# Float32 attention times values for two batches, with row sums from columns of ones, and weight conversion in 512-column pieces

## The chip, the cores and the metric

The kernel runs on one core of one Trainium2 chip. Five engines run their own instruction streams side by side: TensorE (PE in the profile, its weight loads PEld), VectorE (DVE), ScalarE (ACT), GpSimd (POOL) and SyncE (SP), which here issues the DMAs. They wait for each other through semaphores. The metric is the device time of one execution in microseconds (us); the median of several executions counts.

## The reference

Block-causal attention over 8 batches, 8 heads, 576 positions and 64 dimensions, followed by a two-layer feed-forward over all 4608 tokens, everything in float32:

```python
scores = scale * np.matmul(q, k.transpose(0, 1, 3, 2))
scores = np.where(block_i >= block_j, scores, -1000000000.0)      # blocks of 64
scores = scores - np.max(scores, axis=-1, keepdims=True)
attn = np.exp(scores)
attn = attn / (np.sum(attn, axis=-1, keepdims=True) + 1e-09)
x = np.matmul(attn, v)                     # to (4608, 512), heads side by side
h = x @ w_in                               # w_in 512 x 2048
g = np.where(h >= 1, h, np.where(h <= -1, 0.0, (h + 1) ** 2 / 4))
out = g @ w_out                            # w_out 2048 x 512
```

## The kernel before

**Precision.** TensorE multiplies float32 in several passes and a reduced type, float32r, in one. To keep the accuracy, an operand a is split into a high half (a rounded to float32r) and a low half (a minus the high half, again float32r), and a product is the sum of two or three float32r products. So nearly every tile exists twice: `xh` and `xl` for the attention output x, `wih` and `wil` for `w_in`, `gh` and `gl` for the activations g. `w_out` is split once, written to DRAM (`wo_split`) and read back for each use.

**Attention.** The unit is a pair: two heads of one batch, 32 pairs in all, four to a batch. `Pair` holds its methods and `attention_steps` runs each pair in eight steps. Queries are split by `split_q` (its last instruction is on line 292) in the fourth step of the pair before. A head has the score groups (0, 0), (0, 1), (0, 2) for key and query tiles of 128, and both heads share one group for the last 64 positions. For each group `scores` (or `scores_last`) multiplies (lines 371 and 374), takes row maxima (394, DVE), exponentials with their row sums (398, ACT), adds 1e-9 and inverts the sums (`inverse`, 380 and 381), and multiplies the rows of P by them (404, or 430 for the last). `turn` transposes P through PSUM (`transposed`, 441 or 443) and `split` copies it to SBUF: the high half by ACT (434), the low half by DVE (436). `weighted` multiplies it by the values (480).

**Three kinds of batches.** Batch 0 is `plain`: P stays float32, has no low half, and is multiplied by float32 values. The tile `vs` has the values of one head in one half of its columns and zeros in the other, so both heads add up in one PSUM bank (`both`), from which ACT takes `xh` (515) and DVE `xl` (516). All later batches split P in two halves and multiply by `vsr`, which has the high half of the values on one side and their low half on the other; `add_halves` (502 on ACT, 503 on DVE) adds the two sides into `x32`, and `store_x` (545, 546) splits that into `xh` and `xl`. From batch 3 on (`HOP = 3`), P makes a hop through DMA into a float32r tile (`as_float32r`, tile `prr`) before it is transposed, so that the transposes run in float32r. The tiles of a hop come from the pools `conv` and `conv2`, which also serve the weight conversion and the output tiles `ob`.

**Weight conversion.** `convert` splits a piece of 128 rows by `CW = 256` columns in three stages, one for each later step: a load (`bits`), two ACT operations (164, 165) and three DVE operations (166, 169, 172); then an addition on POOL (178) and a copy on ACT (180); then a subtraction on POOL (182). There are 64 pieces. Odd ones among the first 32 borrow tiles from the feed-forward's pool.

**Feed-forward.** Nine chunks of 512 tokens by 16 blocks of 128 hidden columns. A block is `ffn_in`, twelve 512-column matmuls into `ph` (626) and then ACT (635), DVE (636, 639), ACT (640) and POOL (641), and `ffn_out`, twelve more into four banks `po` (650, 655). From step `START = 36`, the middle of batch 1's first pair, one of these half blocks is issued with each attention step, and what is left after the last pair runs alone.

**What sets the order.** The code is written step by step, and a scheduler of the tile framework places the instructions on the engines' queues, by the buffers and operands that each needs. Engines run their queues in order. PSUM has eight banks: three work banks (`ps_w`), one for `ph`, four for `po`. Before `START` the work takes turns over the `po` banks too (`work_bank`), afterwards it has the three alone.

## Time and profile before

| | |
|---|---|
| runs | 1288.21, 1285.29, 1286.38 us; median 1286.38 |
| profiled execution | 1285.23 us, its span 1283.5 us |
| mean granted TensorE clock | 0.983 |
| PE busy | 1207.2 us, 94% of the span |
| PEld busy | 1018.7 us, 79% |
| DVE busy | 888.4 us, 69% |
| ACT busy | 766.3 us, 60% |
| POOL busy | 472.2 us, 37% |
| DMA | 188.44 MB, mean 147 GB/s |

The page divides the span into 40 slices and gives the busy share of each engine in tenths. A row of the grouped views reads: line, engine, operation, output tile <- input tiles, shapes, count | busy us, mean ns of one | idle time of the engine just before, and what ended it. The windows view gives the busy time of every engine between two moments. A row of waits names who waited for whom, the total in us, how often, and the longest.

### The profile page before, as it was taken

What the parts mean: (1) busy time and instruction counts of PE and PEld (TensorE: products, weight loads), DVE (VectorE), ACT (ScalarE), POOL (GpSimd) and SP (SyncE); (2) the same over time, 40 slices, a digit from 0 to 9 for tenths busy, and PEclk for the clock granted to TensorE, in tenths of its full rate; (3) what the DMA queues carried; (4) which work ended last, traced back from release to release, by engine and by line L of the source; (5) the groups of instructions that cost most, each with busy time, mean ns of one, the idle gap of its engine ahead of it and who ended that gap; (6) DMA issues with size and microseconds to landing.
All of it is one profiled execution on the core that took longest, in us unless ns stands there. A gap on an engine that the chain in (4) does not pass through costs nothing.

```text
span 1283.5 us, 20410 instructions
## 1 busy us (share of the span) xinstructions
PE 1207.2 (94%) x6496; PEld 1018.7 (79%) x6496; DVE 888.4 (69%) x2204; ACT 766.3 (60%) x1855; POOL 472.2 (37%) x466
## 2 busy tenths in 40 slices
PE   5877787899999999999999999999999999999998
PEld 4666665688888888888888888888888888888886
DVE  8998999877677777677777777777777767322222
ACT  6878676666666666666666666666666655322222
POOL 3545766633333333333333333333333332222222
PEclk9889999999999999999999999999999999999999
DMA  5656555434333545555444644464545443333432
GB/s 152 175 151 180 170 186 177 145 125 140 97 106 111 189 143 153 160 159 178 147 155 154 187 137 152 153 189 148 159 146 186 156 142 120 115 99 99 132 99 99
DMA packets 136812, 188.44 MB, mean 147 GB/s; under 512 B 61040, under 2 KB 87664, under 8 KB 136704
## 3 DMA queue, kind: packets, MB, share of 16 engines
q1 hardware_dynamic: 136704, 187.13, 47.2%
q8 instruction: 52, 0.85, 0.3%
q14 instruction: 56, 0.46, 0.1%
HBM read 120.59 MB, written 17.83 MB: 108 GB/s over the span
## 4 chain that ended last, share of the span: by engine, by line
PE 70%; DVE 13%; ACT 8%; issue 4%; DMA 2%; POOL 1%; SPq 1%; ACTq 0%; POOLq 0%; DVEq 0%
PE ph L626 26%; PE po L650 16%; PE po L655 8%; PE ps_av L480 7%; PE ps_s L371 3%; PE ps_s L374 3%; ACT pr L398 3%; PE ps_t L441 3%; PE ps_qk L327 2%; DVE pr L404 2%; ACT qb L331 2%; DVE nm L394 2%; DVE work L169 1%; PE ps_t L443 1%; DVE work L172 1%
## 5 line engine op out<-in xcount | busy, mean ns | idle before, releaser
L641 POOL TENSOR_TENSOR gl<-t,gh 128x512 fp32r<-128x512 f32 x144 | 187.2, 1300 | 577.5 <-ACT gh L640 310.8
L650 PE MATMUL po<-wo,gh 128*128 128x512 f32 x1152 | 299.7, 403 | 0.1
L650 PEld LDWEIGHTS po<-wo,gh 128*128 128x128 f32 x1152 | 210.6, 190 | 40.3 <-ACT gh L640 0.6
L626 PE MATMUL ph<-xh,wih 128*128 128x512 f32 x576 | 238.2, 414 | 1.7 <-DVE t L639 1.7
L636 DVE SCALAR_TENSOR_TENSOR t<-t 128x512 f32<-128x512 f32 x144 | 112.9, 784 | 183.1 <-ACT t L635 181.0
L626 PE MATMUL ph<-xl,wih 128*128 128x512 f32 x576 | 227.4, 395 | 1.1 <-DVE xl L516 1.1
L626 PE MATMUL ph<-xh,wil 128*128 128x512 f32 x576 | 227.9, 396 | 0.0
L635 ACT ACTIVATE t<-ph 128x512 f32<-128x512 f32 x144 | 86.0, 597 | 155.2 <-PE ph L626 155.2
L398 ACT ACTIVATE pr<-ps_s,nm 128x128 f32<-128x128 f32 (+3 forms) x256 | 134.2, 529 | 63.1 <-DVE nm L394 62.8
L655 PE MATMUL po<-wo,gl 128*128 128x512 f32 x576 | 155.4, 391 | 0.0
L394 DVE TENSOR_REDUCE nm<-ps_s 128x1 f32<-128x128 f32 (+3 forms) x256 | 123.6, 485 | 45.2 <-PE ps_s L374 43.6
L371 PE MATMUL ps_s<-ka,qa 68*128 68x288 f32 (+4 forms) x384 | 123.6, 336 | 20.5 <-ACT pr L398 12.8
L640 ACT CAST gh<-t 128x512 fp32r<-128x512 f32 x144 | 90.0, 625 | 84.6 <-DVE t L639 83.0
L626 PEld LDWEIGHTS ph<-xh,wil 128*128 128x128 f32 x576 | 109.4, 190 | 24.5
L434 ACT CAST pb<-ps_t 128x512 fp32r<-128x512 f32 (+1 forms) x140 | 77.5, 553 | 84.8 <-PE ps_t L441 65.5
L317 POOL TENSOR_TENSOR vsr<-vn,vsr 128x256 fp32r<-128x256 f32 (+1 forms) x112 | 82.9, 750 | 119.9 <-ACT vsr L316 119.9
L655 PEld LDWEIGHTS po<-wo,gl 128*128 128x128 f32 x576 | 108.4, 188 | 23.4
L626 PEld LDWEIGHTS ph<-xl,wih 128*128 128x128 f32 x576 | 109.9, 191 | 20.4 <-DVE xl L516 1.4
L626 PEld LDWEIGHTS ph<-xh,wih 128*128 128x128 f32 x576 | 109.4, 190 | 20.3 <-DVE t L639 2.0
L374 PE MATMUL ps_s<-kb,qb 128*128 128x288 f32 (+4 forms) x384 | 121.8, 323 | 0.0
L436 DVE TENSOR_TENSOR pb<-ps_t,pb 128x512 fp32r<-128x512 f32 (+1 forms) x140 | 88.1, 629 | 40.5 <-ACT pb L434 40.5
L404 DVE TENSOR_SCALAR pr<-pr,sm 128x128 f32<-128x128 f32 (+3 forms) x256 | 110.3, 451 | 3.6
(95 smaller groups left out, 2039.1 us busy)
## 6 DMA issues: line engine op xcount, KB each, us to landing
wo<-wo_split SPq DMA_DIRECT2D x144, 512.0 KB, 3.4
prr<-pr SPq DMA_DIRECT2D x80, 192.0 KB, 2.6
prr<-pr SPq DMA_DIRECT2D x60, 256.0 KB, 2.4
out_dram<-ob SPq DMA_DIRECT2D x36, 256.0 KB, 4.0
qn<-in_q_dram SPq DMA_DIRECT2D x32, 256.0 KB, 2.9
kn<-in_k_dram SPq DMA_DIRECT2D x32, 256.0 KB, 3.0
bits<-in_moe_w_in_dram SPq DMA_DIRECT2D x32, 256.0 KB, 3.1
bits<-in_moe_w_out_dram SPq DMA_DIRECT2D x32, 256.0 KB, 3.1
```

Source lines behind the costliest of these rows:

```text
L371: nc.tensor.matmul(ps, qa[:KA, j, c0 : c0 + P], ka[:KA, j, k0 : k0 + n], start=first, stop=False)
L374: nc.tensor.matmul(ps, qb[:, j, c0 : c0 + P], kb[:, j, k0 : k0 + n], start=False, stop=last)
L394: nc.vector.tensor_reduce(out=nm[:, i : i + 1], in_=ps[:, cs], axis=AX.X, op=ALU.max, negate=True)
L398: nc.scalar.activation(pr[:, cs], ps[:, cs], AF.Exp, bias=nm[:, i : i + 1], scale=1.0, accum_out=sm[:, i : i + 1],)
L404: nc.vector.tensor_scalar_mul(pr[:, cs], pr[:, cs], sm[:, i : i + 1])
L480: nc.tensor.matmul(ps[:, lo_col:], vt, x, start=first and i == 0 and m == 0, stop=last and i == len(parts) - 1 and m == len(mov) - 1,)
L626: nc.tensor.matmul(ph, w[:, cc, fs], x[:, cc, xs], start=(cc == 0 and i == 0), stop=(cc == NCC - 1 and i == 2),)
L636: nc.vector.scalar_tensor_tensor(out=t_, in0=t_, scalar=1.0, in1=t_, op0=ALU.min, op1=ALU.mult)
L640: nc.scalar.copy(gh, t_)
L641: nc.gpsimd.tensor_tensor(out=gl, in0=t_, in1=gh.bitcast(F32), op=ALU.subtract)
L650: nc.tensor.matmul(po[tt], gh[:, ts_], wo[:, w, :], start=(fc == 0 and w == 0), stop=False)
L655: nc.tensor.matmul(po[tt], gl[:, ts_], wo[:, 0, :], start=False, stop=fc == NFC - 1)
```

## The change

- **Two plain batches.** `PLAIN = 2`: batches 0 and 1 keep P in float32. Batches 2 to 7 hop (`self.hop = not self.plain`), so batch 2 hops too.
- **P unnormalised in plain batches.** The exponentials are neither summed nor divided. The half of `vs` beside a head's values holds ones, so the matmul of P and `vs` gives the weighted sum in one half of the partitions and the row sum in the other. The tiles `vs` and `pc` are made once; their unused rows are zero. The two heads no longer share a PSUM accumulation. The new `divided` copies the sums plus 1e-9 to the other half of the partitions (ACT), inverts them (DVE, 256 or 320 columns) and multiplies (DVE) into `x32`. `store_x` then serves all batches.
- **Evictions.** A P without a low half, in groups 1, 2 and the last, is copied out of PSUM by DVE and no longer by ACT; group 0 stays on ACT.
- **Conversion** in pieces of 512 columns, 32 in all, with the first operations in place. `w_in` lies in four groups of 512 columns, whose last one takes the place of the pool `early` when that closes. Twelve pieces (24 half as large before) are spread over the first 36 steps, then one is issued in each step, two ahead in both cases.
- **Hops** are one DMA each, also for the 576 columns of the last group, into tiles of the one pool `conv` (two tags of two buffers); `ob` takes its tiles from there too.

```diff
-    BORROW = 32
-    CW = 256
+    CW = 512
+    NG = DF // CW
-    HOP = 3
+    PLAIN = 2
...
-    conv = ctx.enter_context(tc.tile_pool(name="conv", bufs=3))
-    conv2 = ctx.enter_context(tc.tile_pool(name="conv2", bufs=3))
+    conv = ctx.enter_context(tc.tile_pool(name="conv", bufs=2))
...
+    late["early"] = late["pool"].enter_context(tc.tile_pool(name="early", bufs=2))
...
+        pool = late["early"] if n % 2 and late["early"] else conv
+        bits = pool.tile([P, CW, 2], I32, tag="bits", name="bits")
+        mag = pool.tile([P, CW], U32, tag="mag", name="mag")
...
-        nc.scalar.mul(top, bits[:, :, 1].bitcast(F32), 2.0**-112)
+        nc.scalar.mul(top, top, 2.0**-112)
...
     def as_float32r(src):
-        for c0 in range(0, src.shape[1], TCH):
...
+        n = src.shape[1]
+        hops["n"] += 1
+        if n > TCH or hops["n"] % 2:
+            dst = conv.tile([P, 2 * TCH], F32R, tag="bits", name="prr")
+        else:
+            dst = conv.tile([P, TCH], F32R, tag="mag", name="prr")
+        nc.sync.dma_start(dst[:, :n].bitcast(F32), src)
...
-            self.plain = b == 0
+            self.plain = b < PLAIN
-            self.hop = b >= HOP
+            self.hop = not self.plain
...
+                    nc.gpsimd.memset(both[:, 0, :, 1, :], 1.0)
+                    nc.gpsimd.memset(both[:, 1, :, 0, :], 1.0)
...
-                    accum_out=sm[:, i : i + 1],
-                )
-            self.inverse(sm[:, :m])
-            for i, cs in enumerate(cols):
-                nc.vector.tensor_scalar_mul(pr[:, cs], pr[:, cs], sm[:, i : i + 1])
+                    accum_out=None if self.plain else sm[:, i : i + 1],
+                )
+            if not self.plain:
+                self.inverse(sm[:, :m])
+                for i, cs in enumerate(cols):
+                    nc.vector.tensor_scalar_mul(pr[:, cs], pr[:, cs], sm[:, i : i + 1])
...
         def split(self, ps, hi, lo=None):
+            if lo is None and ps.shape[1:] == hi.shape[1:] and len(ps.shape) > 2:
+                nc.vector.tensor_copy(hi, ps)
+                return
...
-        def both(self, c0, parts):
...
+        def divided(self, ps, heads, c0):
+
+            n = ps.shape[1] // len(heads)
+            total = att1.tile([P, G1], F32, tag="xtmp", name="xtmp")
+            halves = [slice(j * D, (j + 1) * D) for j in range(2)]
+            for i, j in enumerate(heads):
+
+                nc.scalar.activation(
+                    total[halves[j], :n], ps[halves[1 - j], i * n : (i + 1) * n], AF.Identity,
+                    bias=EPS, scale=1.0,
+                )
+            rows_ = slice(heads[0] * D, (heads[-1] + 1) * D)
+            nc.vector.reciprocal(total[rows_, :n], total[rows_, :n])
+            for i, j in enumerate(heads):
+                nc.vector.tensor_tensor(
+                    out=self.x32[halves[j], c0 : c0 + n], in0=ps[halves[j], i * n : (i + 1) * n],
+                    in1=total[halves[j], :n], op=ALU.mult,
+                )
...
         def attn_v(self, j):
-            if self.plain:
-                return self.both(G0, self.parts) if j else None
             ps = work_bank("ps_av")[:, :G1]
             self.weighted(ps, j, self.parts(j))
-            self.add_halves(ps, j, G0)
+            self.divided(ps, (j,), G0) if self.plain else self.add_halves(ps, j, G0)
...
-        if i < START:
-            want = (i + 1) * EARLY // START
-        else:
-            want = max(
-                EARLY + (i - START + 1) * (NFC // GROUP * PART - EARLY) // (2 * NFC - 4 * GROUP),
-                ((i - START) // (2 * GROUP) + 1) * PART,
-            )
+        want = (i + 1) * EARLY // START if i < START else EARLY + i - START + 1
```

How the queues change, at two places. On DVE in batch 0, where the second head's first groups of a pair are handled, there stood before (`work` is a conversion's tile, `sm` the row sums, `pr` the rows of P):

```order
L380 TENSOR_SCALAR sm<-sm 128x2
L169 TENSOR_SCALAR work<-work 128x256
L381 RECIPROCAL sm<-sm 128x2
L169 TENSOR_SCALAR work<-work 128x256
L404 TENSOR_SCALAR pr<-pr,sm 128x128
L404 TENSOR_SCALAR pr<-pr,sm 128x256
L380 TENSOR_SCALAR sm<-sm 128x1
L172 SCALAR_TENSOR_TENSOR work<-work 128x256
L381 RECIPROCAL sm<-sm 128x1
L172 SCALAR_TENSOR_TENSOR work<-work 128x256
L404 TENSOR_SCALAR pr<-pr,sm 128x384
L394 TENSOR_REDUCE nm<-ps_s 128x1
```

The small sums, their reciprocals and the multiplies of P stand among the conversion. At the same place of the third pair there stands now (`pb` is the transposed P, `ps_t` its PSUM bank, `ps_av` the bank of P times values, `xtmp` the sums, `x` the tile x32, `mag` and `bits` a conversion's tiles):

```order
L540 RECIPROCAL xtmp<-xtmp 64x320
L454 COPY pb_724<-ps_t 128x3x128
L542 TENSOR_TENSOR x_725<-ps_av,xtmp 64x320
L180 SCALAR_TENSOR_TENSOR mag<-bits,mag 128x512
L410 TENSOR_REDUCE nm<-ps_s 128x1 x2
L540 RECIPROCAL xtmp<-xtmp 128x256
L454 COPY pb_724<-ps_t 128x4x128
L542 TENSOR_TENSOR x_725<-ps_av,xtmp 64x256 x2
L410 TENSOR_REDUCE nm<-ps_s 128x1
```

What normalised P before the transposes now divides after the product, in fewer and wider instructions, and the copies of P stand beside them.

On PE in batch 1, the second head's product of P and the values in the pair's last columns was, before:

```order
L480 MATMUL ps_av<-pb_1375,vsr_110 128x320
L480 MATMUL ps_av<-pb_1376,vsr_110 128x320
L480 MATMUL ps_av<-pb_1375,vsr_110 128x320
L480 MATMUL ps_av<-pb_1376,vsr_110 128x320
L480 MATMUL ps_av<-pb_1375,vsr_110 128x320
L480 MATMUL ps_av<-pb_1376,vsr_110 128x320
L480 MATMUL ps_av<-pb_1375,vsr_110 128x192
L480 MATMUL ps_av<-pb_1376,vsr_110 128x192
L480 MATMUL ps_av<-pcs_107,vsr_110 128x64
L480 MATMUL ps_av<-pcs_108,vsr_110 128x64
L626 MATMUL ph<-xh,wih 128x512
```

and is now, with the first feed-forward matmuls behind it in both:

```order
L501 MATMUL ps_av<-pb_1196,vs 128x320 x3
L501 MATMUL ps_av<-pb_1196,vs 128x192
L501 MATMUL ps_av<-pc,vs 128x64
L654 MATMUL ph<-xh,wih_96 128x512
L654 MATMUL ph<-xl,wih_96 128x512
```

Ten float32r matmuls of a high and a low half have become five float32 matmuls. From the fourth batch on the rows of PE, DVE and POOL are the same ones in the same order in both kernels; on ACT a few copies of output tiles stand one or two places later, and on SP the hop of a last group is one DMA where there were two.

More of the change, by code (lines that the diff above doesn't have):

```diff
@@ L505, in add_halves @@
             )
-        def both(self, c0, parts):
-            n = (G0, G1)[c0 > 0]
-            ps = work_bank("ps_av")[:, :n]
-            for j in range(2):
-                self.weighted(ps, j, parts(j), j == 0, j == 1)
-            at = self.b * S + c0
-            hi = xh[:, self.hp, at : at + n]
-            nc.scalar.copy(hi, ps)
-            nc.vector.tensor_tensor(
-                out=xl[:, self.hp, at : at + n], in0=ps, in1=hi.bitcast(F32), op=ALU.subtract
-            )
+        def divided(self, ps, heads, c0):
[13 more added lines that the diff above has]
+                    in1=total[halves[j], :n], op=ALU.mult,
+                )
         def attn_v_first(self):
-            if self.plain:
-                return self.both(0, self.parts_first)
             ps = work_bank("ps_av")
@@ L568, in attention_steps @@
                 cur.turned(False, 1)
-                cur.load("v")
+                if not cur.plain:
+                    cur.load("v")
             if old:
@@ L578, in attention_steps @@
                 old.store_x()
+            if cur and cur.plain:
+                cur.load("v")
             if not cur:
```

124 lines of the change are left out of this document (60 added, 64 removed).

## The prediction

> **What bounds the kernel now.** I read the page's slices first, then cut the span at one recurring instruction and asked for the busy time of each stage.
>
> ```profile
> PE   5877787899999999999999999999999999999998
> PEld 4666665688888888888888888888888888888886
> DVE  8998999877677777677777777777777767322222
> ```
>
> Up to the eighth slice, about 257 us, DVE is the full engine and PE is not; afterwards PE is full. The cut is the query split, one for each pair of heads, issued in the fourth step of the pair before. The second, sixth and ninth stand at 23.6, 109.3 and 253.9 us, the thirteenth at 390:
>
> ```profile
> 109.29 0.73 DVE L292 SCALAR_TENSOR_TENSOR qs<-qn,qs 128x576 fp32r<-128x576 f32 x1
> 253.87 0.75 DVE L292 SCALAR_TENSOR_TENSOR qs<-qn,qs 128x576 fp32r<-128x576 f32 x1
> ```
> ```profile
> 23.60:109.30 85.70, 67.64 (x361) 53.46 (x361) 76.77 (x231) 72.83 (x208) 44.70 (x58) 0.90 0.58 167
> 109.30:253.90 144.60, 113.89 (x566) 91.56 (x564) 132.72 (x306) 100.35 (x269) 92.82 (x105) 0.93 0.55 172
> 253.90:390.00 136.10, 131.69 (x739) 113.58 (x740) 98.39 (x250) 85.34 (x206) 45.66 (x43) 0.99 0.39 117
> 390.00:1031.00 641.00, 636.37 (x3630) 545.83 (x3629) 467.97 (x1190) 415.04 (x986) 219.35 (x197) 1.00 0.51 159
> ```
>
> Columns: length, then busy time (with count) of PE, PEld, DVE, ACT and POOL, then the granted TensorE clock. Stage A, 85.7 us, is four pairs of the first batch without the feed-forward: DVE 76.77 (90%), PE 67.64 (79%). Stage B, 144.6 us, is three pairs with the feed-forward and most of the weight conversion: DVE 132.72 (92%), PE 113.89 (79%) at a clock of 0.93. From 253.9 us a pair costs 136.1/4 = 34.0 us, from 390 us 641/19 = 33.7, with PE busy 97 to 99%. So the sum is made on DVE in A and B, with PE as the floor. What DVE does there, A first, then B:
>
> ```profile
> L404 DVE TENSOR_SCALAR pr<-pr,sm 128x128 f32<-128x128 f32 (+3 forms) x30 | 18.8, 648 | 0.2
> ...
> L166 DVE TENSOR_SCALAR work<-work 128x256 f32<-128x256 f32 x22 | 11.2, 515 | 4.4 <-ACT work L164 4.4
> L172 DVE SCALAR_TENSOR_TENSOR work<-work 128x256 uint32<-128x256 uint32 x21 | 10.5, 501 | 0.1
> L169 DVE TENSOR_SCALAR work<-work 128x256 uint32<-128x256 uint32 x21 | 8.5, 411 | 0.1
> ...
> L381 DVE RECIPROCAL sm<-sm 128x1 f32<-128x1 f32 (+1 forms) x27 | 4.2, 154 | 0.2
> L380 DVE TENSOR_SCALAR sm<-sm 128x1 f32<-128x1 f32 (+1 forms) x27 | 4.0, 147 | 0.7 <-ACT pr L398 0.6
> L516 DVE TENSOR_TENSOR xl<-ps_av,xh 128x256 fp32r<-128x256 f32 (+1 forms) x7 | 3.1, 446 | 1.0 <-ACT xh L515 1.0
> ```
> ```profile
> L172 DVE SCALAR_TENSOR_TENSOR work<-work 128x256 uint32<-128x256 uint32 x39 | 24.4, 629 | 0.5
> L169 DVE TENSOR_SCALAR work<-work 128x256 uint32<-128x256 uint32 x39 | 22.5, 585 | 0.4
> L404 DVE TENSOR_SCALAR pr<-pr,sm 128x384 f32<-128x384 f32 (+3 forms) x25 | 16.7, 688 | 0.1
> L166 DVE TENSOR_SCALAR work<-work 128x256 f32<-128x256 f32 x38 | 14.9, 394 | 2.4 <-ACT work L164 2.3
> ...
> L436 DVE TENSOR_TENSOR pb<-ps_t,pb 128x512 fp32r<-128x512 f32 (+1 forms) x15 | 9.4, 628 | 1.6 <-ACT pb L434 1.6
> ...
> L503 DVE TENSOR_TENSOR x<-ps_av,xtmp 64x320 f32<-64x320 f32 (+1 forms) x12 | 5.4, 452 | 3.3 <-ACT xtmp L502 3.1
> ...
> L381 DVE RECIPROCAL sm<-sm 128x1 f32<-128x1 f32 (+1 forms) x22 | 3.4, 155 | 0.2
> ...
> L436 DVE TENSOR_TENSOR pa<-ps_t,pa 128x384 fp32r<-128x384 f32 x6 | 3.3, 548 | 0.7 <-ACT pa L434 0.7
> L380 DVE TENSOR_SCALAR sm<-sm 128x1 f32<-128x1 f32 (+1 forms) x21 | 3.1, 147 | 0.7 <-ACT pr L398 0.6
> ```
>
> **What goes from DVE.** In both batches the normalising of P and its small reciprocals go: 18.8 + 4.2 + 4.0 in A, 16.7 + 3.4 + 3.1 in B. In A the low half taken straight from PSUM (3.1) moves to POOL, which is half idle there (44.7 of 85.7). In B the low halves of P (9.4 + 3.3) and the adding of halves (5.4) go. Together 30.1 in A and 41.3 in B.
>
> **Conversion.** The nearest rows for 512 columns are these, and they also price what is added:
>
> ```profile
> L636 DVE SCALAR_TENSOR_TENSOR t<-t 128x512 f32<-128x512 f32 x144 | 112.9, 784 | 183.1 <-ACT t L635 181.0
> ...
> L404 DVE TENSOR_SCALAR pr<-pr,sm 128x512 f32<-128x512 f32 x64 | 36.4, 569 | 1.0
> ...
> L381 DVE RECIPROCAL sm<-sm 128x1 f32<-128x1 f32 x160 | 25.0, 156 | 2.8
> ...
> L665 DVE COPY ob<-po 128x512 f32<-128x512 f32 x18 | 12.1, 685 | 4.1 <-PE po L655 3.7
> L381 DVE RECIPROCAL sm<-sm 128x2 f32<-128x2 f32 x64 | 10.4, 163 | 1.7
> ```
>
> A piece is two TENSOR_SCALARs and one two-source operation: 2 x 569 + 784 = 1.92 us at 512 columns. At 256 it costs 1.43 in A (515 + 501 + 411) and 1.61 in B, because DVE meets more company there; I scale the large one by 1.61/1.43 in B, 2.2 us. By the new table 11 pieces fall in A and 18 in B. So 30.2 becomes 21.1 (A) and 61.8 becomes 39.6 (B): 9.1 and 22.2 us off. If the source with a step of two costs DVE its better rate, the two TENSOR_SCALARs go at the 685 of the PSUM copy: 0.23 us a piece, 2.5 and 4 us back.
>
> **What comes to DVE.** Per pair: three PSUM copies of 512 columns (685), two of 384 (548, the same width out of PSUM), a small one of some 0.3: 3.5 us; four multiplies at 452 ns: 1.8 us. In A (four pairs) 14.0 + 7.2, in B (three) 10.5 + 5.4. Then the term I know least: a reciprocal over 256 columns and two over 320 for each pair, where the kernel before has only one and two columns. The two rows differ by 7 ns for one more column. That is the high end: 163 + 254 x 7 = 1.94 us and 2.39 us, 6.7 us a pair. The low end is one column at a time as a PSUM copy goes, (685 - 548)/128 = 1.07 ns: 0.43 and 0.50, 1.4 us a pair. I take the high end, since it is the only row of the operation itself.
>
> The Trainium skill (VectorE: DVE Perf Modes, First, the fixed hardware budget) says that the reciprocal runs through an iterative divide with a repeat count of 8. Read as eight cycles of its 0.96 GHz a column, an estimate from that page, it is 7.9 us a pair and the result would be some 8 us later than my sum; the 2-column row, 7 ns dearer and not 8.3, leaves it open, and both lie in the forecast's own range.
>
> **Stage A.** 76.8 - 30.1 - 9.1 + 14.0 + 7.2 + 26.9 = 85.7 us of DVE; at the 92% that DVE reached in B this takes 93.3, **+7.6**. ACT does not take over: it hands the P copies to DVE and stops reading accumulators, against four short copies a pair.
>
> **Stage B.** 132.7 - 41.3 - 22.2 + 10.5 + 5.4 + 20.2 = 105.3 us of DVE, 115 at 92%. PE is now as near. Its own change:
>
> ```profile
> L480 PE MATMUL ps_av<-pb,vsr 128*128 128x320 f32 x448 | 71.5, 302 | 1.2 <-ACT pr L398 1.2
> L480 PE MATMUL ps_av<-pa,vsr 128*128 128x256 f32 x224 | 31.4, 282 | 0.5 <-DVE pa L436 0.3 <-ACT pr L398 0.2
> ...
> L480 PE MATMUL ps_av<-pb,vs 128*128 128x320 f32 (+1 forms) x64 | 17.5, 417 | 0.6 <-ACT pb L434 0.6
> L480 PE MATMUL ps_av<-pa,vs 128*128 128x256 f32 (+1 forms) x32 | 9.0, 408 | 0.0
> ```
>
> Seven batches of two float32r halves take 102.9 us, 14.7 each; one batch in float32 takes 26.5. So the second batch pays 11.8 us more on PE, 3.0 a pair: 34.0 + 3.0 = 37.0, and 111 us for three pairs is the floor. With two engines at 111 and 105 neither runs free; I take 120 us, PE at 92%: **-24.6**.
>
> **The rest.** The third batch now goes through DRAM to float32r like the later ones: 33.7 instead of 34.0 a pair, **-1.2**. Before A, three pieces stand for four and the first pair loses its normalising: 0 within 2 us. From the fourth batch on PE, DVE and POOL have the same rows in the same order, so nothing is added. Sum: +7.6 - 24.6 - 1.2 = -18.2 on the profiled execution of 1285.2 us, which lies 1.2 under the median 1286.4. **Forecast 1267 us.**
>
> **Rival 1: the wide reciprocal streams.** At 1.4 us a pair DVE has 64.4 us in A and 89.4 in B, and PE is the bound in both: A 67.64/0.95 = 71 (-14.5), B 111/0.95 = 117 (-27.8). Sum -43.5: **1242**. For it: the two reciprocal rows differ by no more than scatter could make. Against: nothing but the same rows.
>
> **Rival 2: the work banks run out.** In the feed-forward stage all transposes, scores and P*v share three PSUM work banks. PE already stops for the one that the adding of halves frees:
>
> ```profile
> PEld ps_t L443 <- DVE x L503: 2.9, 3, 1.8
> PE ps_t L443 <- DVE x L503: 2.5, 3, 1.7
> ```
>
> Each such bank is now held through a reciprocal more, 1.9 to 2.4 us, three times a pair, in the four pairs of the second batch. Queued behind on PE are transposes and then feed-forward matmuls. If PE stands still for all of it, 12 x 2.2 = 27 us come back: 1267 + 27 = **1294**, slower. It decides from 1.6 us a time (19/12). Against: PE stopped six times in B, for 5.4 us in all, while twelve such releases ran.
>
> **Rival 3: the gain is not there.** B is a chain of waits, not a load: conversion has four buffers and later two, where it had five and later three, its pieces come late, PE waits for weights. Then B keeps its 144 us, A its 86: **1285**, within 4. Against: DVE idles only 12 us of B.
>
> **How the numbers follow.** Forecast 48% (1253 to 1280: the reciprocal between 4 and 9 ns a column, B at 114 to 126), rival 1 30%, rival 2 13%, rival 3 9%. A measurement of this kernel tells 0.2%, 2.6 us, from no change. Faster: the forecast, rival 1 and a bit of rival 3, 0.80; same 0.05 (rival 3); slower 0.15. The range takes rival 1 in and stops within rivals 2 and 3: 1240 to 1288; the forecast's own is 1253 to 1280.
>
> **What would show it.** The reciprocal of 64x320: near 2.4 us right, near 0.5 rival 1. DVE in B under 110 us and PE over 90%: the load has moved; both under 85% with waits of ps_t or ps_s on the multiplies: rival 2; waits of ph or po on conversion: rival 3. The distance from the ninth to the thirteenth query split should be 135 us, and the tail unchanged. The forecast is wrong if the pairs of the first batch get shorter than 20 us, or those of the second stay over 45.

## The result and the profile after

| | before | after |
|---|---|---|
| median of 4 runs, us | 1285.84 (1283.99 to 1288.21) | 1295.32 (1294.87 to 1298.23) |
| ratio | | 1.0077, 95% interval 1.0055 to 1.0100 |
| span of the profiled execution, us | 1283.5 | 1293.1 |

The change made the kernel slower by 0.8%, where 1.4% faster was forecast. The page's slices of the changed kernel, in tenths of busy time:

```profile
PE   5677778899999999999999999999999999999998
DVE  7798989767777777777777777777677777322222
```

The change of regime sits where it was before, near the eighth slice. The windows view of the changed kernel, cut at the same query splits (now line 310), has the columns length, busy time and count of PE, PEld, DVE, ACT and POOL, then granted clock, DMA share and GB/s. The stages A, B and C are those of the prediction:

```profile
25.80:129.50 103.70, 76.62 (x382) 60.26 (x383) 88.92 (x152) 69.39 (x128) 40.15 (x30) 0.80 0.48 142
129.50:259.80 130.30, 105.82 (x505) 85.36 (x504) 113.89 (x167) 75.64 (x140) 80.35 (x58) 0.90 0.59 185
259.80:400.40 140.60, 138.40 (x775) 117.88 (x775) 100.04 (x236) 83.25 (x191) 41.49 (x37) 1.00 0.46 142
```

| stage | before, us | after, us | difference | forecast |
|---|---|---|---|---|
| start, to the 2nd split | 23.6 | 25.8 | +2.2 | 0 |
| A, 2nd to 6th split | 85.7 | 103.7 | +18.0 | +7.6 |
| B, 6th to 9th | 144.6 | 130.3 | -14.3 | -24.6 |
| C, 9th to 13th | 136.1 | 140.6 | +4.5 | -1.2 |
| the rest | 893.5 | 892.7 | -0.8 | 0 |

So the saving came from B, as forecast, but smaller, and A and C gave more than all of it back. VectorE's groups in A, the three conversion rows (180, 174, 177) among what is new there:

```profile
L540 DVE RECIPROCAL xtmp<-xtmp 64x320 f32<-64x320 f32 (+1 forms) x12 | 24.1, 2012 | 5.7 <-ACT xtmp L535 5.6
L410 DVE TENSOR_REDUCE nm<-ps_s 128x1 f32<-128x512 f32 (+3 forms) x29 | 13.5, 482 | 7.3 <-PE ps_s L390 7.0
L454 DVE COPY pb<-ps_t 128x512 f32<-128x512 f32 (+1 forms) x19 | 11.5, 606 | 0.1
L180 DVE SCALAR_TENSOR_TENSOR mag<-bits,mag 128x512 uint32<-128x512 uint32 x11 | 8.5, 771 | 0.1
L174 DVE TENSOR_SCALAR bits<-bits 128x512 f32<-128x512 f32 x11 | 7.4, 685 | 0.5 <-ACT bits L172 0.5
L542 DVE TENSOR_TENSOR x<-ps_av,xtmp 64x320 f32<-64x320 f32 (+1 forms) x16 | 7.2, 447 | 0.2
L177 DVE TENSOR_SCALAR mag<-bits 128x512 uint32<-128x512 uint32 x10 | 5.1, 528 | 0.1
```

and in B:

```profile
L180 DVE SCALAR_TENSOR_TENSOR mag<-bits,mag 128x512 uint32<-128x512 uint32 x19 | 19.3, 1018 | 0.3
L540 DVE RECIPROCAL xtmp<-xtmp 64x320 f32<-64x320 f32 (+1 forms) x8 | 16.0, 1996 | 2.2 <-ACT xtmp L535 2.0
L174 DVE TENSOR_SCALAR bits<-bits 128x512 f32<-128x512 f32 x19 | 15.0, 797 | 1.4 <-ACT bits L172 1.4
L177 DVE TENSOR_SCALAR mag<-bits 128x512 uint32<-128x512 uint32 x19 | 14.9, 791 | 1.7 <-POOL wil L190 1.1 <-POOL ws L190 0.4
```

By shape, over the whole run, the reciprocal is:

```profile
L540 DVE RECIPROCAL xtmp<-xtmp 64x320 f32<-64x320 f32 x16 | 34.3, 2145 | 3.7 <-ACT xtmp L535 3.3
...
L540 DVE RECIPROCAL xtmp<-xtmp 128x256 f32<-128x256 f32 x8 | 14.0, 1748 | 6.4 <-ACT xtmp L535 6.4
```

It is the long operation that the prediction had taken (1.94 and 2.39 us forecast, 1.75 and 2.15 measured). VectorE's load came out above the sum that was made for it: 88.9 us in A (85.7 forecast), 113.9 in B (105.3). And the stages were longer than even those loads over 92%. The experiments ask why.

### The profile page after: what moved, and what is told of

It is laid out like the page before. It is cut to its first block, busy times and chain, and to the rows that moved or that the text cites. A ratio compares the mean times of both kernels' runs of the same rounds, so it can differ in the third digit from the quotient of the medians.

```text
span 1293.1 us, 19896 instructions
## 1 busy us (share of the span) xinstructions
PE 1215.0 (94%) x6496; PEld 1023.1 (79%) x6496; DVE 883.3 (68%) x1964; ACT 738.2 (57%) x1627; POOL 452.4 (35%) x386
## 4 chain that ended last, share of the span: by engine, by line
PE 72%; DVE 10%; issue 6%; ACT 6%; DMA 3%; POOL 3%; SPq 0%; ACTq 0%; POOLq 0%; DVEq 0%
PE ph L654 27%; PE po L678 16%; PE po L683 8%; PE ps_av L501 7%; PE ps_s L387 3%; PE ps_s L390 3%; PE ps_t L462 3%; PE ps_qk L345 3%; ACT pr L414 2%; ACT qb L349 1%; POOL mag L186 1%; DVE nm L410 1%; DVE xtmp L540 1%; DMA prr<-pr 1%; DMA bits<-in_moe_w_out_dram 1%
## 5 line engine op out<-in xcount | busy, mean ns | idle before, releaser
L669 POOL TENSOR_TENSOR gl<-t,gh 128x512 fp32r<-128x512 f32 x144 | 188.0, 1305 | 618.0 <-ACT gh L668 368.4
L456 ACT CAST pb<-ps_t 128x512 fp32r<-128x512 f32 (+1 forms) x120 | 66.5, 554 | 77.7 <-PE ps_t L462 76.4
L667 DVE TENSOR_TENSOR t<-ph,t 128x512 f32<-128x512 f32 x144 | 98.4, 684 | 2.1
L335 POOL TENSOR_TENSOR vsr<-vn,vsr 128x256 fp32r<-128x256 f32 (+1 forms) x96 | 72.8, 768 | 75.8 <-ACT vsr L334 75.8
L458 DVE TENSOR_TENSOR pb<-ps_t,pb 128x512 fp32r<-128x512 f32 (+1 forms) x120 | 75.4, 628 | 34.1 <-ACT pb L456 33.9
```

What stands on the lines that cost most here:

```text
L667: nc.vector.tensor_tensor(out=t_, in0=ph, in1=t_, op=ALU.max)
L669: nc.gpsimd.tensor_tensor(out=gl, in0=t_, in1=gh.bitcast(F32), op=ALU.subtract)
```

## The experiments

Three theories stood at the start. Theory 1: stage A is as long as VectorE's work, whose added part is the wide reciprocals. Theory 2: the copies of P on VectorE stand in the way of its short operations. Theory 3: a conversion operation of 512 columns is too long a piece for an engine on which the attention's short operations wait. All variants are edits of the changed kernel. Stage lengths, in us, are taken at the same splits in each variant's profiled execution; the ratio is to the kernel before on the same chip.

| variant | A | B | C | median | ratio, 95% interval |
|---|---|---|---|---|---|
| before | 85.7 | 144.6 | 136.1 | 1285.84 | |
| after | 103.7 | 130.3 | 140.6 | 1295.32 | 1.0077, 1.0055 to 1.0100 |
| e1_no_recip | 78.6 | 132.6 | 140.4 | 1275.13 | 0.9920, 0.9903 to 0.9937 |
| e2_copies_on_act | 106.2 | 127.9 | 140.3 | 1298.34 | 1.0100, 1.0084 to 1.0115 |
| e3_halves | 107.8 | 134.0 | 140.5 | 1307.38 | 1.0176, 1.0156 to 1.0195 |
| e4_one_plain | 106.2 | 138.0 | 136.0 | 1303.04 | 1.0136, 1.0121 to 1.0151 |
| e5_normalised_p | 99.8 | 136.7 | 139.6 | 1298.69 | 1.0105, 1.0090 to 1.0120 |
| e6_hop3 | 106.9 | 127.0 | 139.7 | 1297.26 | 1.0092, 1.0077 to 1.0107 |
| e8_batch0_as_before | 88.3 | 133.0 | 140.1 | 1284.40 | 0.9997, 0.9985 to 1.0008 |
| e9_early20 | 124.7 | 115.2 | 139.6 | 1303.75 | 1.0142, 1.0127 to 1.0157 |
| e10_no_pool_add | 102.3 | 121.1 | 140.2 | 1283.16 | 0.9983, 0.9968 to 0.9998 |
| e11_no_vector_bits | 96.5 | 112.4 | 141.5 | 1268.33 | 0.9864, 0.9847 to 0.9880 |
| e12_seven_pairs | 105.1 | 127.3 | 137.2 | 1289.55 | 1.0040, 1.0024 to 1.0056 |
| e13_combined | 102.1 | 138.8 | 141.3 | 1294.88 | 1.0077, 1.0062 to 1.0092 |
| e14_batch0_and_seven | 88.6 | 133.4 | 138.1 | 1283.04 | 0.9980, 0.9966 to 0.9993 |
| e15_no_recip_no_add | 72.8 | 114.7 | 138.8 | 1249.67 | 0.9723, 0.9709 to 0.9738 |
| e16_two_buffers | 101.2 | 127.1 | 139.9 | 1294.79 | 1.0074, 1.0060 to 1.0088 |

The part of a stage that one profile can tell is about 3 us: variants whose A should be alike (after, e4, e6, e12) have 103.7 to 106.9, those whose B should be alike (after, e2, e6, e16) 127.0 to 130.3. The changed kernel's own profile has the shortest A of the first set and the longest B of the second, so a difference against it can be up to 3 us off.

### The reciprocals: e1

```diff
-            nc.vector.reciprocal(total[rows_, :n], total[rows_, :n])
```

> The wide reciprocal is left out: the plain batches multiply by the row sums instead of dividing. Theory 1 (the wide reciprocals are what slows the changed kernel: 24.1 us of DVE in stage A and 16.0 in stage B, standing between the copies and maxima for which TensorE waits): stage A falls from 103.7 us by 24 or more, to 80 or less, stage B from 130.3 to about 118, and the time from 1295 to about 1260. Theory 2 (the copies of P that moved from ACT to DVE are what TensorE waits for): A stays over 92, the time over 1280. Theory 3 (the longer conversion operations): A stays over 95, since the conversion is untouched.

The windows view of this kernel, stages A and B:

```profile
26.20:104.80 78.60, 63.50 (x367) 50.33 (x367) 63.26 (x135) 60.70 (x117) 39.83 (x29) 0.93 0.55 157
104.80:237.40 132.60, 109.63 (x520) 88.40 (x520) 98.65 (x165) 81.49 (x151) 79.28 (x59) 0.90 0.63 199
```

In A the length falls by 25.1 us, for 25.7 us less of VectorE's work (88.92 to 63.26): the reciprocals count in full. In B 15.2 us less of VectorE's work changed nothing (130.3 to 132.6). So the same operation has two prices, and VectorE's load alone does not set B.

### The copies of P: e2

```diff
-            if lo is None and ps.shape[1:] == hi.shape[1:] and len(ps.shape) > 2:
-                nc.vector.tensor_copy(hi, ps)
-                return
```

> P of the plain batches is copied out of PSUM by ACT again, as in the kernel before; the rest is the changed kernel. Theory 2: the copies (11.5 us of DVE in stage A, 8.8 in B) no longer queue behind reciprocals and conversion, TensorE's waits on the copies go, A falls to about 90 us, the time to about 1280. Theory 1: DVE is relieved by those 20 us but the reciprocals still hold it, A falls by 3 to 6 us, the time to about 1288 to 1292.

A did not get shorter (106.2). Theory 2 falls. The 3 to 6 us of Theory 1 did not come either, and the total of 1298.34 lies above both ranges: with 11.5 us of copies gone VectorE's busy time in A fell by only 3.0 us (88.92 to 85.97), because the three conversion rows, 21.0 us in the changed kernel, have 28.1 here. What lengthened them was not looked into.

### The size of the conversion's operations: e3

```diff
+        cols = [slice(c, c + CW // 2) for c in (0, CW // 2)]
+        for c in cols:
+            nc.scalar.mul(top[:, c], top[:, c], 2.0**-112)
...
-        nc.gpsimd.tensor_tensor(out=w32, in0=w32, in1=low, op=ALU.add)
+        for c in cols:
+            nc.gpsimd.tensor_tensor(out=w32[:, c], in0=w32[:, c], in1=low[:, c], op=ALU.add)
```

> Each operation of the weight conversion is written as two operations on 256 columns, with the 512-column tiles and transfers kept. Theory 1 (stage A is as long as VectorE's work, whose added part is the wide reciprocals) expects no gain: A 102 to 108 us (the fixed part of each operation is paid twice, about 11 pieces x 3 operations x 0.06 us), total 1294 to 1300. Theory 3 (a 512-column operation keeps VectorE or GpSimd long enough to hold up the attention's short operations) expects A 92 to 97 us, B 3 to 5 us shorter, total 1280 to 1286.

Shorter operations made the total longer, by 7 us more than Theory 1 allowed. B grew by 3.7 us, and A is at the upper edge of what Theory 1 said, 1 us above the range of equal kernels. Theory 3 falls: of the two sizes tried here 512 columns is the better one.

### One plain batch: e4

```diff
-    PLAIN = 2
+    PLAIN = 1
...
-            self.hop = not self.plain
+            self.hop = b >= 2
```

> Only batch 0 is plain; batch 1 splits P in two float32r halves and normalises it as before (no hop), batch 2 hops as in the changed kernel. Stage A stays at 103 us. If the float32 product and its reciprocals in batch 1 cost more than the halves did, stage B gets shorter than 130 us and the time falls by as much; if they pay, as the prediction said (DVE 41 us off, 36 on; PE 9 on), B goes back to 135 to 140 and the time to about 1300 to 1305.

With batch 1 in float32r again B is 7.7 us longer and C 4.6 shorter, back at the 136 us of before. The float32 second batch is worth its change in B, and part of it is paid back in C.

### Normalised P: e5

```diff
-            if not self.plain:
-                self.inverse(sm[:, :m])
...
+            self.inverse(sm[:, :m])
...
-            nc.vector.reciprocal(total[rows_, :n], total[rows_, :n])
...
+                nc.vector.tensor_copy(
+                    self.x32[half, c0 : c0 + n], ps[half, i * n : (i + 1) * n]
+                )
```

> P of the plain batches is normalised before the transposes with row sums from the exponentials, as in the kernel before, and the product is copied to x32 by DVE: no wide reciprocal, no ones used, two plain batches and conversion as in the changed kernel. Theory 1: the normalising costs DVE 27 us in stage A as it did before, the reciprocals' 24 go, so A comes out near 100 us or, since the small operations hold nothing up for 2 us, near the 86 of the kernel before; the time 1278 to 1293. Theory 3 (long conversion operations): A stays at 100 or more in any case.

Here P is normalised by the small reciprocals as before, but the copies on VectorE and the copy into `x32` stay. VectorE has 86.87 us in A, nearly as with the wide reciprocals, and A takes 99.8. So it is not the length of the reciprocal that counts in A, but the sum of VectorE's work. The total missed: 1298.69 us where 1278 to 1293 was expected, with B 6.4 us longer than in the changed kernel.

### The hop of the third batch: e6

```diff
-            self.hop = not self.plain
+            self.hop = b >= 3
```

> P of the third batch goes to the transposes as float32 again, as in the kernel before (the rounding by a transfer starts at the fourth batch). If the float32r hop of the third batch costs stage C, C falls from 140.6 to about 136 us and the total to 1290 to 1292. If C's extra 4.5 us come from the last float32 pair, whose second part lies in C, and from work left over from B, C stays at 139 to 143 us, or grows by 1 us as the transposes of float32 take longer, total 1294 to 1298.

C stays (139.7). The hop of batch 2 neither costs nor gains what these runs can tell.

### Batch 0 as before: e8

```diff
+            self.norm = b == 0
...
-            if lo is None and ps.shape[1:] == hi.shape[1:] and len(ps.shape) > 2:
+            if lo is None and not self.norm and ps.shape[1:] == hi.shape[1:] and len(ps.shape) > 2:
...
         def attn_v_first(self):
+            if self.norm:
+                return self.both(0, self.parts_first)
```

> Batch 0 as in the kernel before (P normalised by small reciprocals, zeros beside v, both heads in one bank, copies of P on ScalarE, x split straight from PSUM); batch 1 as in the changed kernel (ones beside v, wide reciprocals); conversion in 512-column pieces. Theory 1 (VectorE's load sets A, and B is set by something else) expects A 77 to 86 us, from a VectorE load of 68 us (76.8 of before less 9.1 for the conversion) at a share of 0.8 to 0.9, B 128 to 132 us, total 1268 to 1277: faster than both kernels. Theory 3 (the 512-column conversion holds up A by itself) expects A 93 us or more and a total of 1283 to 1288.

Stage A of this kernel in the windows view, then VectorE's longest waits in it (waiting engine and line <- awaited engine and line: total us, times, longest):

```profile
25.90:114.20 88.30, 69.58 (x360) 57.71 (x361) 73.68 (x192) 70.55 (x165) 39.17 (x30) 0.79 0.55 160
```
```profile
DVE bits L174 <- ACT bits L172: 5.1, 3, 2.6
DVE xl L563 <- ACT xh L562: 3.0, 3, 1.6
DVE sm L404 <- ACT pr L422: 1.9, 3, 1.2
```

Stage A differs from that of the kernel before in the conversion, in the tile `vs`, which is made once, and in the first scores of the fifth pair, and neither theory hit its length. VectorE's conversion rows have 8.5 us less (8.2 + 7.9 + 5.6 = 21.7 us here, 30.2 before); only 3.1 of it shows in VectorE's busy time, 73.68 us instead of 76.77; and A is 2.6 us longer, as VectorE's idle time went from 8.9 to 14.6 us. TensorE's clock was lower too, 0.79 against 0.90, and its busy time 1.9 us longer; but e14 below, with the same first batch, a clock of 0.83 and TensorE only 0.6 us longer, also has 88.6 us. The cheaper conversion bought nothing here. What the plain P of batch 0 costs stands against this kernel: A 103.7 - 88.3 = 15.4 us.

### Eight more pieces early: e9

```diff
-    EARLY = 12
+    EARLY = 20
```

> 20 instead of 12 conversion pieces are spread over the first 36 steps: 7 more of the 32 lie in stage A, 7 to 8 fewer in B. Theory 1 expects A to grow with VectorE's load, 7 x 2.0 us over a share of 0.86 = 16 us, to 118 to 121 us; B, which did not get shorter when 16 us of reciprocals were taken out, loses 0 to 5 us; total 1304 to 1312. If B is set by the conversion (its VectorE or GpSimd part, or the waits between the two), B falls by 12 to 20 us and the total stays at 1290 to 1299.

The stages A and B in the windows view:

```profile
26.20:150.90 124.70, 86.04 (x389) 65.34 (x389) 108.94 (x176) 80.29 (x149) 61.19 (x45) 0.73 0.53 158
150.90:266.10 115.20, 98.06 (x499) 79.38 (x498) 92.44 (x143) 63.63 (x119) 57.21 (x43) 0.95 0.53 165
```

A grew by 21.0 us, more than Theory 1 said. B fell by 15.1, as it should if the conversion sets it, and the total of 1303.75 lies between the two expectations. By the counts of the conversion rows 8 pieces moved (11 to 19 in A, 19 to 11 in B). At the margin a piece costs A 21.0/8 = 2.6 us and B 15.1/8 = 1.9 us, each up to 0.4 less by the other profiles of equal stages. VectorE's work in A grew by 20.0 us, 2.5 us a piece, where its three operations had taken 0.771 + 0.685 + 0.528 = 1.98 us.

### GpSimd's addition and VectorE's bit operations: e10, e11

```diff
-        nc.gpsimd.tensor_tensor(out=w32, in0=w32, in1=low, op=ALU.add)
```

> GpSimd's addition of the low bits in the weight conversion is left out (the weights lose their low bits): 27.5 us of GpSimd's work in stage B, 16 us in A, nothing of VectorE's. If VectorE's load alone sets B, B stays at 128 to 131 us. If the conversion's round trip between the engines sets it (VectorE to GpSimd to ScalarE to GpSimd, which removing 16 us of reciprocals left as it was), B falls by 8 us or more, to 122 us or less. For A, where the reciprocals counted in full, both expect 98 to 104 us. Total 1285 to 1295 by VectorE's load, 1275 to 1285 by the round trip.

VectorE's reciprocals and conversion rows in B of this kernel:

```profile
L539 DVE RECIPROCAL xtmp<-xtmp 64x320 f32<-64x320 f32 (+1 forms) x8 | 16.0, 1996 | 3.2 <-ACT xtmp L534 3.2
L180 DVE SCALAR_TENSOR_TENSOR mag<-bits,mag 128x512 uint32<-128x512 uint32 x19 | 15.9, 842 | 0.2
L174 DVE TENSOR_SCALAR bits<-bits 128x512 f32<-128x512 f32 x19 | 12.5, 668 | 1.5 <-ACT bits L172 1.4
L177 DVE TENSOR_SCALAR mag<-bits 128x512 uint32<-128x512 uint32 x19 | 11.7, 625 | 1.3 <-POOL wil L189 1.1
```

B fell by 9.2 us, at least 5.9 by the other profiles of an equal B. GpSimd lost work, and VectorE's unchanged operations became shorter: 40.1 us instead of 49.2 for the same 19 pieces, 9.1 us. A GpSimd operation of the conversion thus costs VectorE time without standing in VectorE's queue. The Trainium skill (Trainium Architecture — The Big Picture, What this means for kernel authors) says that VectorE and GpSimd share one pair of ports under an exclusive lock; the 1018 ns that become 842 ns agree with it, though they can't tell a lock from a shared rate.

```diff
-        nc.vector.tensor_scalar(
-            out=mag, in0=top.bitcast(U32), scalar1=3, scalar2=None, op0=ALU.logical_shift_left
-        )
-        nc.vector.scalar_tensor_tensor(
...
-        nc.gpsimd.tensor_tensor(out=w32, in0=w32, in1=low, op=ALU.add)
+        nc.gpsimd.tensor_tensor(out=w32, in0=top.bitcast(I32), in1=low, op=ALU.add)
```

> Two of the three VectorE operations of each conversion piece are left out (the shift and the sign, so that the weights are other numbers): 34.2 us of VectorE's work in B, 13.6 us in A. VectorE's load expects A at 86 to 90 us (13.6 us over a share of 0.86 less) and B at 105 to 113 us, where TensorE's own 106 us end it; total 1255 to 1262. If B is set by the conversion's round trip through GpSimd and ScalarE, or by its transfers, B keeps 120 us or more, total 1267 or more.

B reached 112.4 us, as VectorE's load expected, but A fell only 7.2 of the 14 to 18 us, so that the total of 1268.33 is that of the other side. The pieces also fell differently, 13 instead of 11 in A and 16 instead of 19 in B, which is part of both differences. GpSimd's addition in B, in the changed kernel and then in this one:

```profile
L186 POOL TENSOR_TENSOR mag<-mag,bits 128x512 int32<-128x512 int32 x19 | 27.5, 1448 | 14.1 <-DVE mag L180 9.8 <-issue 3.1 <-POOL gl L669 0.7
```
```profile
L179 POOL TENSOR_TENSOR mag<-bits 128x512 int32<-128x512 int32 x16 | 17.6, 1103 | 3.9 <-DVE bits L174 1.3 <-ACT ws L181 1.0 <-ACT bits L173 0.9
```

It fell from 1448 to 1103 ns. The edit changes that addition's source as well; the subtraction into `ws`, which it leaves alone, fell from 1522 to 1305 ns in the same stage. In B the two engines lengthen each other.

### The last float32 pair: e12

```diff
-            self.plain = b < PLAIN
+            self.plain = b * NPAIR + hp < 7
```

> The eighth pair, the last of batch 1, has P normalised and split into float32r as the pairs from batch 2 on; the first seven stay float32. If C's extra 4.5 us are that pair's float32 products, which lie in C where TensorE is busy 98% of the time, C falls to 136 to 137 us, B grows by 1 to 4 us (its scores and transposes are normalised and split again), total 1291 to 1296. If C's time comes from elsewhere (work that B left over), C stays at 139 to 141 us.

Stage C of this kernel in the windows view:

```profile
259.40:396.60 137.20, 135.34 (x771) 115.89 (x770) 99.88 (x254) 87.21 (x208) 44.71 (x41) 1.00 0.50 158
```

C fell by 3.4 us and PE's work in it by 138.40 - 135.34 = 3.1 us. The float32 products of the eighth pair lie in C, and PE, busy for 98% of it, has no room there. B did not grow, and the total of 1289.55 lies a little below the 1291 to 1296 expected.

### Versions meant to beat both: e13, e14

Both take batch 0 from e8, whose edits are left out here, and the eighth pair from e12.

```diff
-            self.plain = b < PLAIN
+            self.plain = b * NPAIR + hp < 7
+            self.norm = b == 0
...
-    EARLY = 12
+    EARLY = 9
...
-        want += LAG
+        want += LAG if i >= 3 else -LAG - EARLY
```

> A version meant to beat both: batch 0 as in the kernel before (as in e8_batch0_as_before), pairs 5 to 7 with float32 P and wide reciprocals, pair 8 float32r again, 9 conversion pieces instead of 12 over the first 36 steps, and none of them issued in the first three. From the single changes: start 23.5 to 25 us (if the early pieces caused its 2.3 us more), A 80 to 84 us (88.3 less 2.6 pieces x 2 to 3 us), B 135 to 140 us (133 plus 2.6 pieces x 2.1 us, plus the split of pair 8), C 136 to 137 us; total 1272 to 1281. If the effects do not add (the work only moves on to the next stage), 1282 to 1287.

The start, A, C and the total missed. The second split came at 15.5 us, not at 23.5 to 25, so the early pieces do hold up the start; but the pair behind it, where the three held-back pieces come together, took 28.1 us (17.8 in e8), and the sixth split came at 117.5 us (114.2 in e8). At the other end the last piece now falls into C, which gained nothing from its pair in float32r.

```diff
-            self.plain = b < PLAIN
+            self.plain = b * NPAIR + hp < 7
+            self.norm = b == 0
```

> Batch 0 as in the kernel before, pairs 5 to 7 with float32 P and wide reciprocals, pair 8 float32r again; conversion as in the changed kernel (12 pieces over the first 36 steps). If the single effects add (A 88.3 us without the wide reciprocals, C 3.4 us shorter and B 3 us shorter with pair 8 as before): start 26, A 88, B 128 to 133, C 137, total 1276 to 1281. If the gain of B only moves, as in the combination with fewer early pieces, 1283 to 1288.

Without the shift of pieces it is 1283.04 us, ratio 0.9980, interval 0.9966 to 0.9993: faster than the kernel before by 0.2%, just more than can be told, and than the changed one by 0.9%. A kept the 88 us, C gained 2.0 of the 3.4 us, B nothing, so that the effects do not add in full; the total is at the lower edge of the second expectation.

### What ends B: e15, e16

```diff
-            nc.vector.reciprocal(total[rows_, :n], total[rows_, :n])
...
-        nc.gpsimd.tensor_tensor(out=w32, in0=w32, in1=low, op=ALU.add)
```

> Both the wide reciprocals and GpSimd's addition of the low bits are left out (batches 0 and 1 are multiplied by the sums instead of divided, the weights lose their low bits). Alone, the reciprocals' removal left B at 132.6 us and the addition's at 121.0. If the conversion's way through GpSimd hid the reciprocals in B, B now falls clearly below 121 us, to 105 to 114. If B without the addition is set by TensorE with its waits, whatever VectorE does, B stays at 117 to 123 us. A by both: 76 to 80 us, total 1254 to 1268.

Stage B of this kernel in the windows view:

```profile
98.30:213.00 114.70, 102.64 (x526) 81.86 (x526) 87.17 (x165) 81.87 (x152) 52.44 (x40) 0.99 0.73 232
```

114.7 us is just above the range for a hidden load, and below that for TensorE alone; A (72.8) and the total came out below theirs. In B the reciprocals were worth nothing with the addition in place and 121.1 - 114.7 = 6.4 us without it; the addition was worth 9.2 us with the reciprocals and 132.6 - 114.7 = 17.9 without. So each hides part of the other. This is what two chains of nearly the same length would do, VectorE's queue and the conversion's way through GpSimd; that the chains are these two is argued from the edits and not traced wait by wait. PE, busy for 102.6 of the 114.7 us, is close behind.

```diff
-        pool = late["early"] if n % 2 and late["early"] else conv
+        pool = conv
```

> The two extra buffers of the first 24 conversion pieces are not used: two pieces in flight throughout instead of four. If the way of a piece (its transfer of 4.5 us and its turns between the engines) with few buffers is what B waits for, as the last 8 pieces already have only two, B grows by 5 us or more and A by 5 us or more, total 1305 or more. If VectorE's and GpSimd's work, and not the buffers, set the length, A and B stay within 3 us of 103.7 and 130.3, total 1291 to 1300.

Half the buffers for the early pieces changed nothing (1294.79 us). The number of the conversion's buffers is not what A or B waits for.

## Why the prediction was wrong

**What bounds the kernel: right in A, half right in B.** In A VectorE is the engine that sets the length: with the wide reciprocals gone A fell by as much as they had taken. In B the prediction let the load pass from VectorE to PE. e1 shows that VectorE's load alone does not set B, e10 and e15 that the conversion's work on GpSimd has a part in it.

**The steps that failed.** Both stages were worked out in two steps: row times are taken off VectorE's busy time and others added (85.7 and 105.3 us), and the result is divided by a share of about 92%. Both steps failed, the first in A and B, the second in A.

*Row times are not busy time.* Records of VectorE overlap: the first of these two, from the kernel before, ends at 23.69 us, after the second has begun (start, length, instruction):

```profile
23.28 0.41 DVE L301 CAST ks<-kn 128x512 fp32r<-128x512 f32 x1
23.62 1.29 DVE L292 SCALAR_TENSOR_TENSOR qs<-qn,qs 128x576 fp32r<-128x576 f32 x1
```

A row counts both in full, the busy time counts the common moment once. All of VectorE's rows add up like this:

| | rows before, us | rows after | change | change forecast | busy before | busy after | change |
|---|---|---|---|---|---|---|---|
| A | 91.8 | 96.3 | +4.5 | +8.9 | 76.77 | 88.92 | +12.15 |
| B | 150.3 | 123.8 | -26.5 | -27.4 | 132.72 | 113.89 | -18.83 |

As rows the forecast was near, in B by luck (below). But with many short instructions replaced by fewer long ones (231 to 152 in A, 306 to 167 in B) the overlap shrank, from 15.0 to 7.4 us in A and from 17.6 to 9.9 in B. So removing the small operations freed 7.6 and 7.7 us less of VectorE than their rows say. e5 shows the same from the other side: with the small operations back and the reciprocals gone, the rows of A are 5.6 us longer than in the changed kernel (101.9), and the busy time is 2 us shorter (86.87).

**Stage A, +7.6 forecast, +18.0 measured: 3.2 us of the difference are load, 7.2 us are the "92% that DVE reached in B".** The load is 7.6 us more by the lost overlap and 4.4 less by the rows. VectorE was busy for 86% of A. It idles 14.8 us there, where the forecast left it 7.6. This is not a share: in the changed kernel and its variants A runs from 72.8 to 124.7 us, but VectorE's idle time in it only from 13 to 20, and in the kernel before it was 8.9. In the changed kernel the largest parts are 7.0 us of waits for scores (2.1 before) and 5.6 for ScalarE's copies of the sums, a wait that the new reciprocal brings; the forecast counted neither.

The experiments split the 18.0 us by cause. e1 against the changed kernel: the reciprocals cost 25.1 us, where 26.9/0.92 = 29.2 was forecast. e1 against e8, whose stages A differ in the normalising, the copies, the multiplies and the step of two heads to one bank: 88.3 - 78.6 = 9.7 us gained, where (30.1 - 14.0 - 7.2)/0.92 = 9.7 was forecast. That these agree to a tenth is luck, with 3 us between equal stages. e8 against the kernel before: the conversion cost 2.6 us, where it was to gain 9.1/0.92 = 9.9. Here the two failed steps show best. "30.2 becomes 21.1 (A)" came true as rows, 21.0 us in the changed kernel and 21.7 in e8; but in e8 8.5 us of rows gone are 3.1 us of busy time, and VectorE's idle time grew by 5.7. That growth stands before three operations, and most of it is waiting for ScalarE: 6.7 us instead of 4.4 before the conversion's first, 3.1 instead of 1.0 before the low half of x, 2.1 instead of 0.7 before the sums. Why it comes with the new conversion stays open: with operations of half the width (e3) or half the early buffers (e16) VectorE idles 14.0 and 13.4 us of A, about as much as in the changed kernel.

**Stage B, -24.6 forecast, -14.3 measured: 8.6 of the 10.3 us are load, 113.9 us instead of 105.3.** The overlap is 7.7 of them. The rows hit by luck, as two errors cancel. The mis-sized term is the conversion's, "2.2 us" a piece: it is 1018 + 797 + 791 ns = 2.6 us, so 19 pieces take 49.2 us where 18 were to take 39.6. GpSimd's part in that shows in e10, where a piece takes 2.1 us without the addition. Against it the reciprocals took 16.0 us, eight of 2.0, and not the 20.2 of nine of 2.2, and other rows were smaller too. The step "I take 120 us, PE at 92%" fell with the load: neither PE, with 105.8 us (the floor of 111 was too high), nor VectorE, with 113.9, is busy for 92% of the 130.3 us.

**Stage C, -1.2 forecast, +4.5 measured: a term left out.** The 3.0 us that a float32 pair costs PE were right (e12: 3.1), but batch 1 has four pairs, and the eighth pair's products fall in C, where nothing hides them: e12 shows 3.4 of the 5.7 us. The hop's -1.2 us did not show (e6). The rest is within what one profile can't tell.

**The start, 0 within 2 forecast, +2.2 measured.** e13 shows that conversion pieces of the first steps stand in its way, but not that 512-column pieces do so more than 256-column ones. That stays open.

**The rivals.** Rival 1 is out by the reciprocal's own row. Rival 2's wait is small. It was so before: the six stops of 5.4 us are three, each listed for PE and for its weight loads at the same moment, 2.5 us on PE. In the changed kernel PE waited in B for banks that the multiplies free 3.7 us and 1.7 us, and without the reciprocals B was no shorter (e1). The waits view of the changed kernel, stage B:

```profile
PE ps_t L464 <- DVE pb L454: 4.0, 2, 3.5
PE ph L654 <- DVE t L667: 3.9, 1, 3.9
PE ps_qk L345 <- ACT pr L414: 3.7, 1, 3.7
PE ps_t L464 <- DVE x L542: 3.7, 2, 1.9
...
PE ps_qk L345 <- DVE x L542: 1.7, 1, 1.7
```

The measured 1295 is rival 2's 1294 by chance, not by its mechanism. Rival 3 said that B is a chain of waits round the conversion: its condition was the nearest to what the runs show, but its price, no gain at all, was not, and its buffers were not the reason (e16). Of the signs, the reciprocal of 64x320 stood near 2.4 us (2.15), while B, with VectorE busy for 113.9 us and PE for 81%, fits none of the three that were set for it. The pairs of the first batch took 25.9 us and those of the second 43.4, inside the bounds of 20 and 45: those signs were too wide to show this miss.

**The reciprocal's price per column.** The Trainium skill (VectorE: DVE Perf Modes, First, the fixed hardware budget) gives the divide a repeat count of 8, which was read as eight cycles of 0.96 GHz, 8.3 ns, a column. The two shapes differ by (2145 - 1748)/64 = 6.2 ns a column, so the trace does not bear out that reading; the row of the small reciprocals, 7 ns a column, was nearer.

## What to carry to other kernels

Do not take the row times of many short instructions off an engine's busy time: their records overlap, and here 7 to 18 us of a stage's rows were no busy time of their own. Do not carry an engine's share of one stage over to another; look at what its idle time waits for. Busy time saved on the fullest engine shortens a stage only if the stage's other chains are shorter too: price a piece of side work by moving some of it between stages (here 2.6 and 1.9 us), not by its durations. Work on GpSimd can belong on VectorE's bill, as an operation there lengthened VectorE's own here. And book each added operation to the stage in which it runs: a reciprocal that cost nothing in one stage cost its full length in another, and the last unit of a change can run in a stage that has no slack.

## What the runs showed of the hardware

- The reciprocal on VectorE took 1748 ns for 128x256 and 2145 ns for 64x320. The mean over its 8 instances in B is 1996 ns with GpSimd's additions and 1996 ns without them (e10), where the conversion's three operations fell by 129 to 176 ns: the additions do not lengthen the reciprocal, but they do lengthen those.
- A TENSOR_SCALAR that reads every second column of its source was no slower than one that reads them all. Over the changed kernel the shortest of lines 174 and 177, with a step of two, took 407 and 408 ns for 512 columns; in the kernel before the conversion's on 256 columns without a step took 264 and 267 at the shortest (lines 166 and 169), and the one of the query split on 512 (line 291) 409 on average from 390 us to 1031. In the first 25.8 us of the changed kernel, with GpSimd busy for 7.5 us, the three conversion operations took:

```profile
L180 DVE SCALAR_TENSOR_TENSOR mag<-bits,mag 128x512 uint32<-128x512 uint32 x3 | 2.0, 682 | 0.0
L174 DVE TENSOR_SCALAR bits<-bits 128x512 f32<-128x512 f32 x3 | 1.5, 498 | 1.9 <-ACT bits L172 1.8
L177 DVE TENSOR_SCALAR mag<-bits 128x512 uint32<-128x512 uint32 x3 | 1.3, 424 | 0.1
```

  That is 1.6 us a piece, below the 1.92 forecast; in B the same three take 2.6 us.
- TensorE's granted clock in A varied between 0.73 (e9) and 0.93 (e1, e15). The length of A does not follow it alone: at 0.79 A took 88.3 us in e8 and 106.9 in e6, and at 0.90 it took 85.7 in the kernel before. What the clock adds to A was not separated.
